# Top-k attention and a low-rank mixer on one core: the pace of the parameter conversion, two reciprocals, one step's masks and one tile's buffer

## The chip, the cores and the metric

The kernel runs on 1 core of one Trainium2 chip. The metric is the device time of one execution in microseconds (us); lower is better. Engines are named as in the profile: PE is the matrix engine, PEld its weight loads, DVE the vector engine, ACT the scalar engine, POOL the GpSimd engine, SP the queue that issues most DMAs.

## The reference

```python
# attention: batch 8, heads 8, seq 576, head_dim 64
scores = (1 / np.sqrt(64)) * np.matmul(q, k.transpose(0, 1, 3, 2))
kth = np.partition(scores, -32, axis=-1)[..., -32:-31]        # 32nd largest of a row
scores = np.where(scores >= kth, scores, -1e9)
attn = np.exp(scores - scores.max(-1, keepdims=True))
attn = attn / (attn.sum(-1, keepdims=True) + 1e-9)
out = np.matmul(attn, v)
# bridge: (B,H,S,D) -> x of (B,S,H*D) = (8, 576, 512)
# mixer: U (576,32), V (32,576), w_ch1 (512,2048), w_ch2 (2048,512)
h = x.transpose(0, 2, 1) @ U @ V
u = x + h.transpose(0, 2, 1)
result = u + np.maximum(u @ w_ch1, 0.0) @ w_ch2
```

q, k and v are float32. The four mixer parameters arrive as float64 and are handed to the kernel as pairs of 32-bit words, so that the kernel itself turns them into float32.

## The kernel before, in words

**Work units.** The heads of a batch are taken in pairs: a pair `g` is two heads of one batch, 4 pairs a batch (`NPAIR = 4`), 32 in all. The 576 query rows of a pair are cut into four tiles of 128 rows (`t` = 0 to 3) and a tail of 64 (`t = 4`). One tile has two lanes (its two heads), each of 128 rows by 576 scores; the tail of both heads together is one lane, `Stail`.

**Steps.** An outer loop over `n` runs through the list `steps`. In the first batch every tile and every tail is a step of its own, 5 a pair, so that steps 0 to 19 are the first batch (`ALONE = 20`). From step 20 on a pair has 4 steps, and the last of them holds tile 3 and the tail together, three lanes; it is called a border step here. Steps 23, 27, 31 and so on are border steps: 28 in all.

**What a step does to a tile.** PE makes the scores of the *next* step's tile (L350), ACT copies them to `Ssb` (L395, L404 to L406). DVE finds each row's 32nd largest by four rounds of an 8-fold maximum (L521, L539) with three removals between (L534); from pair 5 on it first folds the two halves of a row with POOL's help (`fold` and `split`: POOL L446 adds the halves, DVE L448 takes their maximum straight from the scores' PSUM buffers, POOL L449 subtracts), and then works on halves of 288 (L500, L502) and 304. Then come the masks: ACT scales the threshold (`least`, L565), writes a large number wherever a score is below it (L571, tile `E`), and POOL subtracts that from the scores (L572). ACT then takes the exponential and the row sum (`weigh`, L453; sums in `den`). The weights are turned, on PE (L634, L639) up to pair 5 and by DVE (L598) and a trip through DRAM after that, and PE multiplies them by V (L708, L711; copied out by ACT L720). When a pair is done, `inverse` makes the reciprocals of its sums on DVE (L651, L653) and sends them to DRAM, `scale` fetches them back spread over the partitions, POOL multiplies by them (L740, L743), and the mixer's small products follow (`mixed`).

**Order.** The instructions stand in the order in which the loop writes them, on each engine in that order; nothing moves them later. Each step's tile is followed by a generator, `front`, whose parts (`next(here)` for this step's tile, `next(last)` for the tile before) the loop calls in turn. The two-layer product of a finished batch (`mlp`, PE L845 and L862) is cut into single matmuls and dealt out between these parts by `fill`.

**Parameters.** A list `params` of 36 blocks is worked off by `next_params(1)`: each call finishes one block (DVE shift by 3 bits, L202 or L193; POOL adds L203 and L205), starts the ACT passes of the block before it (L179, L180, L183; single ones are also dealt out by `fill`) and issues the DMA of a new one (L157) into one of three `raw` buffers. With fewer than `LATE` blocks left, the shift takes the two-input form L193 instead of L202. The first batch's loop calls it twice in tiles 0 and 1, once in tiles 2 and 3; from step 20 on the calls stand behind the scores (L1312) and behind `split`.

**Buffers.** Tag `E` has two buffers. The third lane's mask goes into tag `tplace`, which has one.

Of the kernel before, what the change touches and what calls it, by code (L numbers as in the profile page):

```python
# [26 lines left out]
def kernel(  # L27
# [30 lines left out]
    P = 128  # L58
# [81 lines left out]
        return slice(h * D, (h + 1) * D)  # L140

    SLAB = 512
    LATE = 12
    spare = []


# [85 lines left out]
    def next_params(n):  # L232

        while passes:
            passes.pop(0)()
        while parts:
            f64_join(*parts.pop(0))
        while raws:
            r, outs = raws.pop(0)
            if isinstance(outs, list):  # L240
                parts.append((*f64_parts(r, None), outs))
                continue
            made = f64_parts(r, outs)
            parts.append((*made, [(made[1], same)]))
        for _ in range(min(n, len(params))):
            srcs, outs = params.pop()
            raws.append((f64_raw(srcs), outs))
# [186 lines left out]
    def split(g, t):  # L434

        if (g, t) in folds:
            pair(g, t, 1)
# [30 lines left out]
    def front(tiles):  # L468
# [92 lines left out]
        if gaps:  # L561
            slots = [lane[0] for lane in gaps]
            lo, hi = min(slots), max(slots) + 1
            least = small.tile([P, 3], F32, tag="least", name="least", bufs=3)
            nc.scalar.mul(least[:, lo:hi], m8[:, lo:hi, 7], WIDEN)  # L565
            for c, chunk, *_ in gaps:
                if c == 2:
                    gap = attn.tile([P, S], F32, tag="tplace", name="E", bufs=1)
                else:
                    gap = attn.tile([P, S], F32, tag="E", name="E")  # L570
                nc.scalar.activation(gap, chunk, AF.Relu, bias=least[:, c : c + 1], scale=-WIDEN)  # L571
                nc.gpsimd.tensor_tensor(chunk, chunk, gap, ALU.subtract)  # L572
            yield
# [615 lines left out]
    def tiles(n):  # L1189

        return steps[n] if 0 <= n < STEPS else []
# [22 lines left out]
        pass  # L1214
    scores(0, 0)
    turning = ready = iter(())
    fronts = {}
    for n in range(STEPS + 2):
        if n < STEPS:
            g, t = steps[n][0]  # L1220
            if t == 0 and g < NPAIR:
                load(g + 1)
            if t == (1 if g < NPAIR else 2) and g + 1 < NP:
                ready = prep(g + 1)
            fronts[n] = front(steps[n])
            next(fronts[n])
        else:
            t = NT
        here, last = fronts.get(n, iter(())), fronts.pop(n - 1, iter(()))
        if n >= ALONE - 1 and n <= ALONE:  # L1230

            if n < ALONE:
                next(last)
                values(*steps[n - 3][0])
                list(turning)
                next(here)
                next(last)
                scores(*steps[n + 1][0])
                fold(*steps[n + 1][0])
                values(*steps[n - 2][0])  # L1240
            list(turns(*steps[n - 1][0]))
            values(*steps[n - 1][0])
            if n < ALONE:
                split(*steps[n + 1][0])
                next(here)
                next(here)
                inverse(g, 0, 2 * NT)
                mixing.append(mixed(g, 1))
                fill()
                next(here)  # L1250
                continue
            fill()
            scores(*steps[n + 1][0])
            fold(*steps[n + 1][0])
            next(here)
            while mixing:
                fill()
            next_params(1)
            fill()
            next(last, None)  # L1260
            next(here)
            fill()
            split(*steps[n + 1][0])
            next(here)
            coming = loading(g + 1)
            next(coming)
            next(coming)
            next(here)
            fill()
            continue  # L1270
        if n < ALONE:
            ease = n > 0 and eased(*steps[n - 1][0])
            if ease:
                next(last, None)
            scores(*steps[n + 1][0])
            fold(*steps[n + 1][0])
            if n >= 3:
                values(*steps[n - 3][0])
                if (n - 3) % CH == NT:
                    mixing.append(mixed((n - 3) // CH, 3))  # L1280
            list(turning)
            fill()
            next(here)
            if t < NT - 1:
                next_params(1)
            fill()
            next(ready, None)
            next(here)
            next(last, None)
            fill()  # L1290
            split(*steps[n + 1][0])
            next(here)
            if t in (0, 1, NT - 1):
                next_params(1)
            next(here)
            fill()
            if n >= 1:
                turning = turns(*steps[n - 1][0])
            continue
        next(last, None)  # L1300
        fill()
        if ALONE <= n - 3 <= STEPS - 3:
            weighted(n - 3)
            if waiting:
                waiting.clear()
                if next(mixing[0], True):
                    mixing.pop(0)
        for tile_ in tiles(n + 1):
            if tile_[1] < NT:
                scores(*tile_, len(tiles(n + 1)) > 1)  # L1310
            fold(*tile_)
        next_params(1)  # L1312
        turn()
        fill()
        turn()
        next(last, None)
        for tile_ in tiles(n - 2):
            back(*tile_)
        fill()
        turn()  # L1320
        fill()
        next(last, None)
        if n < STEPS and n - 2 >= ALONE and len(tiles(n - 2)) > 1:
            scale(steps[n - 2][0][0])
        next(here, None)
        fill()
        if n >= STEPS:
            if n == STEPS:
                inverse(NP - 1, 0, 2 * NT + 1)
                scale(NP - 1)  # L1330
            weighted(n - 2)
        next(here, None)
        for tile_ in tiles(n + 1):
            split(*tile_)
        if t < NT - 1:
            next_params(1)
        fill()
        next(here, None)
        for tile_ in tiles(n - 1):
            if shared(*tile_):  # L1340
                blocks(*tile_)
        turning = turned(n - 1)
        if n < STEPS and n - 1 >= ALONE and len(tiles(n - 1)) > 1:
            inverse(steps[n - 1][0][0], 0, 2 * NT + 1)
        if n < STEPS:
            if t == NT - 1:
                coming = loading(g + 2) if g + 2 < NP else iter(())
            next(coming, None)
        next(ready, None)
        next(here, None)  # L1350
        fill()
        fill()
# [35 lines left out]
```

## Time and profile before

| what | value |
|---|---|
| time, three runs | 1660.09, 1662.59, 1664.67 us; median 1662.59 |
| profiled execution: time, span | 1663.47 us, 1661.4 us |
| mean granted PE clock | 0.966 |
| PE, DVE busy | 1562.3 us (94%), 1550.0 us (93%) |
| ACT, POOL busy | 991.2 us (60%), 1012.4 us (61%) |
| DMA | 189.42 MB, mean 114 GB/s |

The page cuts the span into 40 slices of 41.5 us. In the first five (the first batch) PE shows 4 to 7 tenths and the clock 7 tenths, DVE 9 from the second on; from the twelfth to the 36th PE and DVE both show 9 tenths. Then DVE falls to between 2 and 5 tenths and PE goes on alone: the last batch's two-layer product (`closing`).

### The profile page before, as it was taken

Reading aid. Unit: us, or ns where it says so; the run is one execution under the profiler, and the core shown is the slowest. Engines: PE = TensorE matmul, PEld = TensorE weight load, DVE = VectorE, ACT = ScalarE, POOL = GpSimd, SP = SyncE. Lnnn points to the kernel's source line nnn. Section 1 sums busy time; section 2 is a strip of 40 time slices with the busy share of each in tenths; the row PEclk is TensorE's granted clock in tenths of the full one; section 3 lists DMA queues with packets and bytes.
Section 4 is the critical chain, followed back from the end, with each engine's and each line's share of the span. In section 5 each row is a group of like instructions: output and inputs, shape, how many; then the busy total and the mean of one; then the engine's idle time right before and its main releaser. Section 6 shows DMA issues by size and latency. Waiting matters only on the chain.

```text
span 1661.4 us, 30244 instructions
## 1 busy us (share of the span) xinstructions
PE 1562.3 (94%) x9638; PEld 1188.0 (72%) x9638; DVE 1550.0 (93%) x4394; ACT 991.2 (60%) x2475; POOL 1012.4 (61%) x881
## 2 busy tenths in 40 slices
PE   4676698999899999999999999999999999999999
PEld 2444466787677887778777887788777877788776
DVE  7999999999999999999999999999999999994452
ACT  4888778665555666566665656566665656564320
POOL 4787669666656565666666565656666565653620
PEclk7777798999999999999999999999999999999999
DMA  3323232244545555454445555454545455543001
GB/s 88 90 82 94 67 95 74 57 128 128 136 126 140 139 144 138 133 138 131 129 130 137 132 152 133 131 138 129 131 128 140 129 154 132 134 123 110 8 2 29
DMA packets 280399, 189.42 MB, mean 114 GB/s; under 512 B 174288, under 2 KB 261168, under 8 KB 280240
## 3 DMA queue, kind: packets, MB, share of 16 engines
q1 hardware_dynamic: 259728, 117.62, 29.3%
q10 hardware_dynamic: 20512, 69.87, 13.3%
q8 instruction: 76, 1.25, 0.3%
q14 instruction: 83, 0.68, 0.1%
HBM read 116.49 MB, written 70.91 MB: 113 GB/s over the span
## 4 chain that ended last, share of the span: by engine, by line
PE 69%; DVE 20%; DMA 3%; POOL 3%; ACT 2%; SPq 2%; issue 1%; ACTq 0%; DVEq 0%; POOLq 0%
PE mm L862 22%; PE mm L845 19%; DVE m L539 7%; PE sc L350 6%; DVE upper L534 6%; PE O L711 6%; PE mm L938 3%; DVE first L521 2%; PE tp L938 2%; PE sc L938 2%; PE sc L382 2%; PE up L785 2%; DVE y L598 1%; PE O L708 1%; DVE place L534 1%
## 5 line engine op out<-in xcount | busy, mean ns | idle before, releaser
L845 PE MATMUL mm<-uT,w 128*128 128x320 f32 (+1 forms) x1792 | 465.3, 411 | 3.0 <-POOL uT L801 2.3
L862 PE MATMUL mm<-hT,w 128*128 128x320 f32 (+1 forms) x1792 | 462.0, 409 | 0.0
L572 POOL TENSOR_TENSOR Ssb<-Ssb,E 128x576 f32<-128x576 f32 x243 | 341.3, 1424 | 195.2 <-ACT E L571 195.2
L845 PEld LDWEIGHTS mm<-uT,w 128*128 128x128 f32 x1792 | 335.7, 192 | 104.2 <-issue 12.8
L862 PEld LDWEIGHTS mm<-hT,w 128*128 128x128 f32 x1792 | 333.6, 191 | 92.6 <-issue 11.1
L539 DVE MAX8 m<-upper 128x8 f32<-128x304 f32 (+1 forms) x774 | 362.7, 509 | 0.7
L534 DVE MATCH_REPLACE8 upper<-m,upper 128x304 f32<-128x304 f32 (+1 forms) x516 | 256.8, 505 | 0.0
L446 POOL TENSOR_TENSOR lower<-Ssb 128x576 uint32<-128x576 uint32 x108 | 152.8, 1415 | 133.3 <-ACT Ssb L395 71.3
L449 POOL TENSOR_TENSOR lower<-lower,upper 128x576 uint32<-128x576 uint32 x108 | 152.3, 1410 | 130.2 <-DVE upper L448 128.0
L453 ACT ACTIVATE Ssb<-Ssb,nmax 128x576 f32<-128x576 f32 x258 | 201.7, 784 | 19.4 <-POOL Ssb L545 9.8
L350 PE MATMUL sc<-qkT 64*128 64x288 f32 (+1 forms) x1056 | 177.7, 459 | 9.8 <-ACT Ssb L404 7.9
L571 ACT ACTIVATE E<-Ssb,least 128x576 f32<-128x576 f32 x243 | 176.2, 768 | 4.3
L502 DVE MAX8 upper<-lower 128x8 f32<-128x288 f32 x432 | 172.0, 439 | 4.4 <-POOL lower L449 4.4
L395 ACT COPY Ssb<-sc 128x576 f32<-128x576 f32 x216 | 127.5, 642 | 75.7 <-PE sc L350 75.7
L598 DVE STREAM_TRANSPOSE y<-Ssb 128x512 f32<-128x512 f32 (+1 forms) x312 | 154.1, 545 | 0.3 <-ACT Ssb L453 0.2
L711 PE MATMUL O<-PT,va 128*64 128x128 f32 x2048 | 143.8, 284 | 0.0
L857 ACT ACTIVATE hT<-mm 128x320 f32<-128x320 f32 (+1 forms) x224 | 91.1, 408 | 81.7 <-PE mm L845 77.5
L350 PEld LDWEIGHTS sc<-qkT 64*128 64x128 f32 (+1 forms) x1056 | 95.7, 197 | 50.1 <-issue 17.5
L711 PEld LDWEIGHTS O<-PT,va 128*64 128x64 f32 x2048 | 112.6, 140 | 16.1 <-issue 1.6
L720 ACT COPY XT<-O 128x128 f32<-128x128 f32 x128 | 34.0, 266 | 113.1 <-PE O L711 108.3
L534 DVE MATCH_REPLACE8 upper<-first,upper 128x304 f32<-128x304 f32 x216 | 97.5, 459 | 0.0
L500 DVE MATCH_REPLACE8 lower<-upper,lower 128x288 f32<-128x288 f32 x216 | 94.0, 443 | 0.0
(268 smaller groups left out, 2271.6 us busy)
## 6 DMA issues: line engine op xcount, KB each, us to landing
away<-y SPq DMA_DIRECT2D x416, 144.0 KB
PT<-away ACTq DMA_DIRECT2D x104, 576.0 KB
raw<-in_moe_w_ch_dram SPq DMA_DIRECT2D x32, 512.0 KB
va<-in_v_dram SPq DMA_DIRECT2D x64, 128.0 KB
scale<-rd ACTq DMA_DIRECT2D x56, 144.0 KB
out_dram<-ob SPq DMA_DIRECT2D x59, 128.0 KB
ld<-in_q_dram SPq DMA_DIRECT2D x108, 64.0 KB
ld<-in_k_dram SPq DMA_DIRECT2D x108, 64.0 KB
```

The lines of the kernel that those rows point to most:

```text
L350: nc.tensor.matmul(out, lhsT=qkT[half(h), 0, cols(t)], rhs=qkT[half(h), 1, lo:hi], start=True, stop=True,)
L446: nc.gpsimd.tensor_tensor(bottom, a.bitcast(U32), b.bitcast(U32), ALU.add)
L453: nc.scalar.activation(E, chunk, AF.Exp, bias=nmax, scale=SCALE, accum_out=total)
L502: nc.vector.max(spot, lower)
L534: nc.vector.match_replace(nxt, ms[c], curs[c], NEG)
L539: nc.vector.max(ms[c], curs[c])
L571: nc.scalar.activation(gap, chunk, AF.Relu, bias=least[:, c : c + 1], scale=-WIDEN)
L572: nc.gpsimd.tensor_tensor(chunk, chunk, gap, ALU.subtract)
L598: nc.vector.transpose(y[:, :, i * NT : i * NT + c].rearrange("p r c j -> p c r j"), E2[:, a : a + c * P].rearrange("p (c r j) -> p c r j", ...
L711: nc.tensor.matmul(O[half(h)], lhsT=va[:, h, j, :], rhs=PT[:, NT * h + j], start=False, stop=(j == NT - 1),)
L845: nc.tensor.matmul(phs[f][:, 0:w], lhsT=first_layer(cc, f), rhs=uT[:, cc, lo:hi], start=(cc == 0), stop=(cc == NC - 1),)
L862: nc.tensor.matmul(po[:, 0:w], lhsT=w2[:, f, c * P : (c + 1) * P], rhs=hTs[f][:, 0:w], start=(f == 0), stop=(f == NF - 1),)
```

## The change

It has five parts. (1) `next_params` is called twice in tile 2 of the first batch too (seven blocks a pair instead of six), three times in step 20 instead of once, and from step 21 on at other places: behind `next(here)` instead of behind the scores, and at the step's end instead of behind `split`, with step 23's first call left out. (2) `LATE` goes from 12 to 8. (3) The `inverse` of pairs 4 and 5 moves from the end of a step to behind the first part of the next step's `front`. (4) In step 24 the masks of step 23 (`next(last)`) move from the head of the step to behind the second `turn()`. (5) The third lane's mask takes a buffer of tag `E` like the others.

```diff
-    LATE = 12
+    LATE = 8
...
             for c, chunk, *_ in gaps:
-                if c == 2:
-                    gap = attn.tile([P, S], F32, tag="tplace", name="E", bufs=1)
-                else:
-                    gap = attn.tile([P, S], F32, tag="E", name="E")
+                gap = attn.tile([P, S], F32, tag="E", name="E")
                 nc.scalar.activation(gap, chunk, AF.Relu, bias=least[:, c : c + 1], scale=-WIDEN)
                 nc.gpsimd.tensor_tensor(chunk, chunk, gap, ALU.subtract)
...
-    fronts = {}
+    fronts, owed = {}, []
...
             next(fronts[n])
+            if owed:
+                inverse(owed.pop(), 0, 2 * NT + 1)
...
             split(*steps[n + 1][0])
+            next_params(1)
             next(here)
             coming = loading(g + 1)
             next(coming)
             next(coming)
+            next_params(1)
             next(here)
...
-            if t in (0, 1, NT - 1):
+            if t < NT:
                 next_params(1)
...
-        next(last, None)
+        slow = n == ALONE + NT
+        if not slow:
+            next(last, None)
         fill()
...
             fold(*tile_)
-        next_params(1)
         turn()
         fill()
         turn()
         next(last, None)
+        if slow:
+            next(last, None)
...
         next(here, None)
+        border = g == NPAIR and t == NT - 1
+        if not border:
+            next_params(1)
         fill()
...
         for tile_ in tiles(n + 1):
             split(*tile_)
-        if t < NT - 1:
-            next_params(1)
         fill()
...
         if n < STEPS and n - 1 >= ALONE and len(tiles(n - 1)) > 1:
-            inverse(steps[n - 1][0][0], 0, 2 * NT + 1)
+            owed.append(steps[n - 1][0][0])
+            if owed[0] > NPAIR + 1:
+                inverse(owed.pop(), 0, 2 * NT + 1)
...
         next(ready, None)
+        if t != 0:
+            next_params(1)
         next(here, None)
```

## The prediction

> **What bounds the kernel.** I read the stretches first, then the waits, then the timeline from 240 to 340 us. Columns of the stretches: us, then busy time of PE, PEld, DVE, ACT and POOL, granted PE clock, DMA share, GB/s.
>
> ```profile
> 206.00:236.00 30.00, 29.30 (x158) 20.14 (x159) 30.00 (x57) 28.84 (x66) 21.59 (x17) 1.00 0.36 106
> 248.80:253.00 4.20, 0.04 (x1) 0.04 (x1) 4.20 (x12) 2.88 (x7) 1.82 (x2) 0.79 0.00 0
> 253.00:258.00 5.00, 5.00 (x13) 3.44 (x14) 5.00 (x15) 5.00 (x12) 5.00 (x4) 0.50 0.00 0
> 258.00:282.00 24.00, 23.84 (x165) 17.40 (x163) 22.51 (x66) 22.44 (x53) 23.61 (x18) 1.00 0.44 127
> 282.00:289.00 7.00, 4.50 (x13) 2.78 (x13) 5.21 (x16) 5.26 (x12) 6.77 (x8) 0.76 0.00 0
> 289.00:331.00 42.00, 41.90 (x285) 30.69 (x284) 38.67 (x119) 25.68 (x65) 28.73 (x24) 1.00 0.21 49
> 400.00:440.00 40.00, 33.90 (x220) 24.50 (x219) 39.97 (x124) 22.57 (x59) 25.54 (x24) 0.96 0.58 154
> 500.00:1500.00 1000.00, 999.04 (x6400) 772.81 (x6401) 997.28 (x3032) 604.12 (x1532) 618.71 (x538) 1.00 0.51 135
> ```
>
> Up to about 250 us DVE is the bound (184.83 of 186 us from 20 to 206, 30.00 of 30 above). From 500 to 1500 PE never waits, and its long matmuls start every 269 or 216 ns almost without spread: PE is the bound, and DVE keeps up by 2.7 us in 1000. Whatever the change does early arrives at the end only as an earlier PE. PE's losses are in 248 to 289 and 400 to 440 us. This is where the change works:
>
> ```profile
> 250.09 0.21 ACT L565 ACTIVATE least<-m 128x3 f32<-128x3 f32 x1 [7.07 <-DVE m L539]
> 252.96 1.11 PE L634 MATMUL tp<-ident,Ssb 128*128 128x128 f32 x4 [4.18 <-ACT XT L720]
> ...
> 258.46 1.73 POOL L205 TENSOR_TENSOR w<-w,raw 128x512 uint32<-128x512 uint32 x1
> ...
> 261.60 0.82 DVE L502 MAX8 upper<-lower 128x8 f32<-128x288 f32 x2 [0.54 <-POOL lower L449]
> ...
> 284.18 0.44 PE L750 MATMUL tp<-ident,uT 128*128 128x128 f32 x2 [2.01 <-POOL uT L740]
> ...
> 287.00 0.82 DVE L502 MAX8 upper<-lower 128x8 f32<-128x288 f32 x2 [1.79 <-POOL lower L449]
> ...
> 331.03 0.76 DVE L448 TENSOR_TENSOR upper<-sc,Ssb 128x576 f32<-128x576 f32 x1 [2.15 <-ACT Stail L415]
> ```
>
> ACT stands 7.07 us before step 23's masks, which need DVE's last maximum; the copy that PE wants (L720) is queued behind them, so PE stands 4.18 us and then runs at half clock from 251.23 to 258.05. From 258 to 282 POOL is 98% busy (23.61 of 24): conversion adds (L203, L205) delay its folds, for which DVE waits, and L740, for which PE waits. At 331 DVE waits for PE.
>
> **Masks of step 23 behind two turns.** ACT's copies L720, L395 and L635 no longer stand behind L565; the masks still start when DVE is done, since ACT is idle until then. PE's 4.18 us go, and with them the half clock: 5.1 us of work at half speed, 2.55 us. But PE then meets the next gate: the scores at 262.77 need the PSUM buffers that DVE's L448 frees, which ended at 258.44. PE's work between is 9.81 − 2.55 = 7.26 us, so PE would be there at about 257 and wait. PE's gain at this point is therefore set by DVE, 262.77 against L448's new end.
>
> **Seven blocks a pair.** DVE does four more L202 before step 20, 4 × 0.41 = 1.64 us later (ends 0.40 and 0.85 each, the extremes in that stage), fully on the path, DVE being the bound there. Up to L448 of step 24 the order of before has six L193: 1.75 + 0.82 + 0.67 + 0.67 + 1.36 + 1.47 = 6.74 us. After, all eight that are left (LATE 8) stand ahead of it.
>
> ```profile
> L193 DVE SCALAR_TENSOR_TENSOR w<-w,nought x12: 667/1091/1751, 210.7 to 290.7; 128x512 uint32<-128x512 uint32 x12
> L202 DVE TENSOR_SCALAR w<-w x20: 399/408/852, 51.1 to 203.5; 128x512 uint32<-128x512 uint32 x20
> ```
>
> L193 costs 0.67 alone and about 1.45 where it starts beside POOL's mask subtracts, soon after a step's first maxima. The new places are behind the second maxima and at the step's end; I take 0.9, nearer to the rows in mid-step (258.37, 269.98, 281.60: 0.68). So 8 × 0.9 − 6.74 = +0.46, with 1.64 makes L448 of step 24 2.1 us later, at 260.5; PE starts the scores there, **2.2 us earlier** than before. Ends: at 0.67 4.1 us earlier, at 1.45 2.2 us later. The added ACT passes (two blocks of 0.68 + 0.77 + 0.77, 4.4 us more before 250) lie in the 7.07 us in which ACT stood; POOL's two pairs of adds (5.2 us) in the 8.4 us that it has free from 206 to 236. SP's `raw` DMAs wait for L205 and hold the loads behind them; the loads of pair 5 are needed at 232, so I take nothing.
>
> **Relief behind step 24.** Before, six more L193 (0.68 + 1.45 + 0.68 + 1.44 + 0.68 + 1.59 = 6.5 us) and seven pairs of POOL adds stood behind 257 us; after, no L193 and one pair. L740 then need not wait for 281.72's add, and PE's 2.01 + 0.26 + 0.22 us at 284 go, as does the half clock from 285.36 to 288.77 (1.7 us): **4.2 us**. If L740 stays late, this is nought. DVE gets ahead by its L193 and its waits for L449 (0.54 + 0.92 + 1.79), 9.8 us in all, but what PE has not won it gives back at 331, where it waits for PE already.
>
> **The clock.** Idle times of 4.18, 2.5 and 2.26 us were each followed by half clock (6.83, 3.41, 3.41 us), those of 1.06 and 1.27 at 405 and 417 were not. The new wait of up to 3.5 us before 260.5 can bring one, 1.7 to 2.55 us; ACT and POOL, fuller before 250, may stretch PE's work over it and prevent it. I charge half of the smaller: 0.85 us.
> The Trainium skill (TensorE: Matmul & The Clock Gate, "What's actually happening") has the clock fall after an idle window of about 3.4 us. The drops after 2.5 and 2.26 us speak against taking this as a threshold for one wait; by the rule the 1.7 us at 285 would have another cause and the estimate would be that much smaller.
>
> **Reciprocals.** One DVE wait ends (0.84 us before L651 at 311.55; there is none at 260.62), worth nothing at the end since DVE waits for PE at 331. The four DMAs to DRAM start some 4 us later (260.62 against L521's end at 264.7), on SP behind four more loads that were out by 265 before; pair 4's fetch may then hold ACT's queue by up to 2 us (issue at 268.41), with L640 and two L857 behind it, whose buffers PE needs only 8 us later (32 matmuls of 269 ns). Nothing.
>
> **The third mask in tag E.** It must wait for POOL's first subtract:
>
> ```profile
> 629.95 1.44 ACT L571 ACTIVATE E<-Ssb,least 128x576 f32<-128x576 f32 x2
> 630.80 2.79 POOL L572 TENSOR_TENSOR Ssb<-Ssb,E 128x576 f32<-128x576 f32 x2 [3.37 <-ACT E L571]
> 631.29 0.76 ACT L571 ACTIVATE E<-Stail,least 128x576 f32<-128x576 f32 x1
> ```
>
> The subtract ends at 632.22, so ACT stands 0.92 us, in all 28 border steps alike, with L857 (or L873), L720 and L395 behind it. In this step ACT idles 0.41 + 0.42 us before L720 and L395 anyway, and PE reused the buffer that L857 frees 3.73 us after its end (3.1 to 11.4 in the others, but one of 0.87 at 353.6); POOL's L446 starts at 634.91 behind the third subtract, not behind L395. I take 0; the other end is 0.92 × 28 = 26 us.
>
> **The sum.** 2.2 + 4.2 − 0.85 = 5.6 us. The profiled execution (span 1661.4 in 1663.47 us) comes to 1657.9; it lay 0.88 us above the median of before, so the median comes to **1657.0 us**.
>
> **Rivals.**
> *DVE's early load eats it.* L193 stays at 1.45 beside POOL, and the new PE wait costs the full half clock: −2.2 + 4.2 − 2.55 = −0.6, about 1663; between this and the forecast lies 1660. For it: POOL is fuller before 250 than before. Against: the new places.
> The Trainium skill (SBUF — State Buffer, "SBUF: two separate sides") says that VectorE and GpSimd lock a shared port pair for a whole instruction and that the other blocks; by that each of the eight could wait out a 1.3 us add, an estimate of up to 2 us each and a loss.
> *The E ring turns the sign.* ACT's 0.92 us less the 0.42 that it idles reach PE in each border step: 0.5 × 28 = 14 us, 14 − 5.6 = 8.4 slower, 1671. It decides from (5.6 + 5) / 28 = 0.38 us a step. For it: PE is the bound there with no slack of its own. Against: the 3 to 11 us of buffer slack.
> *More than forecast.* PE's idle from 400 to 440 (6.1 us, for DVE's and POOL's results) goes too: 1651. Against: DVE is tied to PE at 331.
> That the change does not do what it says can be excluded: the instruction orders show each move, and PE's order is the same in both.
>
> **Numbers.** Forecast 0.53, early load 0.27, E ring 0.15, more 0.05. About 0.3% (5 us) is what a measurement of this kernel can tell from no change. The forecast lies just beyond it (1657.6), as does the larger gain: faster 0.58; early load same 0.27; slower 0.15. The range runs from L193 at 0.67 with no half clock (1.9 + 0.85 more: 1654) and part of the 400 us idle, 1652.5, to the early load's end with a little from the ring, 1664.
>
> **What would show it.** Right: no PE wait above 1 us at step 24's first L634, PE idle below 0.5 us at L750 of pair 4, at most one half clock between 245 and 290 us, L193 x8 near 0.9 us, DVE's wait before 331 longer than 2.15 us, PE busy throughout from 500. Wrong: L193 above 1.3 us, PE waits for L720 or L857 in the border steps, or DVE idle before 250 us.

## The result

The changed kernel takes 1664.87 us (median of 22 runs, 1662.43 to 1668.36), the kernel before 1661.91 us in 22 runs on the same chips: ratio 1.0019, 95% interval 1.0012 to 1.0025, so 3.0 us slower. The forecast was 5.6 us faster; sign and range were missed. The profiled execution has a span of 1663.4 us against 1661.4. From L571 of the kernel before up to its loop, lines of the changed kernel are 3 lower: L571, L720 and L857 are L568, L717 and L854 there. The experiments keep the numbers of the kernel that they start from, and those with the third mask back in `tplace` have the numbers of the kernel before.

The same stretches as before, for the changed kernel (us, then busy time of PE, PEld, DVE, ACT and POOL, granted PE clock, DMA share, GB/s):

```profile
206.00:236.00 30.00, 25.08 (x123) 16.55 (x122) 26.82 (x52) 24.45 (x55) 21.49 (x17) 0.89 0.44 119
248.80:253.00 4.20, 4.20 (x29) 3.13 (x29) 4.20 (x11) 2.23 (x5) 1.39 (x1) 1.00 0.01 1
258.00:282.00 24.00, 20.18 (x126) 14.58 (x125) 21.28 (x70) 14.79 (x37) 19.12 (x14) 0.86 0.13 33
282.00:289.00 7.00, 7.00 (x45) 5.12 (x42) 6.02 (x16) 4.64 (x12) 4.15 (x6) 1.00 0.00 1
500.00:1500.00 1000.00, 998.42 (x6393) 769.96 (x6392) 998.10 (x3035) 604.66 (x1534) 619.70 (x538) 1.00 0.52 136
```

The two places that the change aimed at are clean: PE is busy throughout at 248.8 to 253 and at 282 to 289, though these are stretches of time, and the changed kernel is some 7 us later in its work there. New holes are at 206 to 236, where DVE, the bound of that stretch, fell from 30.00 busy us to 26.82, and at 258 to 282, where PE fell from 23.84 to 20.18 at a clock of 0.86. The steady state is as before.

To place the loss, I compare the start of each step between the two traces: DVE's first maximum of step n, and PE's scores issued in step n (times of before; changes in us, each against before's profiled execution).

```
                        DVE L521, step   20      21      25  |  PE scores L350, issued in step 24   25      26     60
kernel before (us)                    199.1   209.4   263.9  |                             262.8  275.5   291.8  687.8
changed kernel                        +1.2    +7.1    +7.3   |                             +7.5   +7.1    +2.4   +2.4
three calls -> one in step 20         +1.1    +1.1    +1.1   |                              0.0   -0.1    -4.6   -5.4
... and masks at head of step 24      +1.1    +1.1    +1.3   |                             +3.1   +2.7    -2.0   -2.0
... and masks behind the copies       +1.4    +1.4    +1.4   |                             -5.8   +1.6    -3.1   -3.2
... and POOL clear for the subtracts  +1.5    +1.5    +0.4   |                             -3.7   -2.1    -5.2   -4.8
before + masks behind the turns       +0.1    +0.1    +1.9   |                             +4.0   +3.6    +0.7   +0.6
before + masks behind the copies      -0.2    +0.5    +1.3   |                             -7.4   +4.0    +0.9   +0.5
before + masks, POOL clear            +0.2    +0.2    +0.1   |                             -3.8   -1.3    +0.1   +0.3
before + two calls in step 20         +0.1    +7.0    +8.9   |                             +8.2   +8.9    +6.9   +6.3
```

From the third row down the kernels are the experiments that follow ("..." adds to the third row's kernel). The changed kernel loses 5.9 us within step 20 and wins 4.7 us between 275 and 292 us; from there on its distance stays between 1.9 and 3.4 us, 2.4 in the last step. Each row is one execution. That of the kernel before took 1663.47 us, 1.6 above its median, so that the others look faster in the rows by about that much; how long a kernel takes is read from the medians.

Step 20 in the changed kernel's timeline (start, us, engine, line; in brackets the idle time before and what ended it):

```profile
204.69 1.19 DVE L202 TENSOR_SCALAR w<-w 128x512 uint32<-128x512 uint32 x1
...
209.22 0.28 ACT L406 COPY Ssb<-sc 128x128 f32<-128x128 f32 x1
...
210.83 0.69 ACT L179 ACTIVATE w<-raw 128x512 f32<-128x512 f32 x1
...
211.56 0.69 DVE L193 SCALAR_TENSOR_TENSOR w<-w,nought 128x512 uint32<-128x512 uint32 x1 [2.90 <-ACT w L179]
...
214.95 1.63 DVE L193 SCALAR_TENSOR_TENSOR w<-w,nought 128x512 uint32<-128x512 uint32 x1
...
216.50 1.41 DVE L521 MAX8 first<-Ssb 128x8 f32<-128x576 f32 x2
...
217.05 0.67 ACT L179 ACTIVATE w<-raw 128x512 f32<-128x512 f32 x1 [2.33 <-DMA raw<-in_moe_w_ch_dram]
...
219.84 0.74 ACT L854 ACTIVATE hT<-mm 128x320 f32<-128x320 f32 x2
...
220.31 1.97 PE L842 MATMUL mm<-uT,w 128*128 128x320 f32 x3 [4.31 <-ACT hT L854]
```

`next_params` is a line of three stations: a call runs the shift (L193) of the block that the call before converted, starts ACT's passes of the block that the call before fetched, and fetches the next. The middle call therefore puts an L193 into DVE's order whose input (L179) ACT makes only at 210.83, behind the score copies L404 to L406 and two copies of `uT`. DVE, in order, stands 2.90 us with all its maxima behind it. The step's growth adds up: L202 at 1.19 instead of 0.41 (0.78; it runs beside POOL's L755, and takes 0.41 again in the kernel with one call), the wait (2.90), and two L193 that the kernel before has in later steps (0.69 and 1.63) make 6.00 us; 7.1 − 1.2 = 5.9 were measured. The third call has its own wait: its data have not landed, ACT stands 2.33 us for them before 217.05, the copy L854 is queued behind, and PE stands 4.31 us before 220.31, with 6.83 us of half clock from 218.56.

Step 24 in the changed kernel's timeline:

```profile
256.30 1.29 POOL L203 TENSOR_TENSOR w<-w,raw 128x512 uint32<-128x512 uint32 x1 [3.27 <-DVE w L193]
...
257.67 1.29 POOL L205 TENSOR_TENSOR w<-w,raw 128x512 uint32<-128x512 uint32 x1
...
258.93 1.40 POOL L446 TENSOR_TENSOR lower<-Ssb 128x576 uint32<-128x576 uint32 x1
...
260.29 3.22 POOL L569 TENSOR_TENSOR Ssb<-Ssb,E 128x576 f32<-128x576 f32 x2
...
261.72 0.78 ACT L568 ACTIVATE E<-Stail,least 128x576 f32<-128x576 f32 x1 [2.88 <-POOL Ssb L569]
...
262.40 0.76 ACT L453 ACTIVATE Ssb<-Ssb,nmax 128x576 f32<-128x576 f32 x1
...
263.31 0.43 ACT L854 ACTIVATE hT<-mm 128x320 f32<-128x320 f32 x1
...
263.79 4.64 PE L842 MATMUL mm<-uT,w 128*128 128x320 f32 x8 [3.81 <-ACT hT L854]
263.81 0.73 DVE L448 TENSOR_TENSOR upper<-sc,Ssb 128x576 f32<-128x576 f32 x1
...
268.88 0.82 DVE L502 MAX8 upper<-lower 128x8 f32<-128x288 f32 x2 [2.69 <-POOL lower L449]
```

PE's 4.18 us at the transpose are gone, and 3.81 us at the next product have come: the third mask and the weighing (L453) wait on ACT for POOL's subtracts, those stand behind two conversion adds and the fold of the next step (L446), and the copy that PE needs (L854) stands behind the weighing. L448 ends only after PE has resumed; it isn't what PE waits for.

### The profile page after: what moved, and what is told of

It is laid out like the page before. It is cut to its first block, busy times and chain, and to the rows that moved or that the text cites. A ratio compares the mean times of both kernels' runs of the same rounds, so it can differ in the third digit from the quotient of the medians.

```text
span 1663.4 us, 30247 instructions
## 1 busy us (share of the span) xinstructions
PE 1561.3 (94%) x9638; PEld 1185.0 (71%) x9638; DVE 1547.4 (93%) x4394; ACT 992.9 (60%) x2475; POOL 1011.2 (61%) x881
## 4 chain that ended last, share of the span: by engine, by line
PE 70%; DVE 21%; DMA 3%; ACT 2%; POOL 2%; SPq 1%; issue 1%; DVEq 0%; ACTq 0%; POOLq 0%
PE mm L859 22%; PE mm L842 20%; DVE m L539 7%; PE sc L350 7%; DVE upper L534 6%; PE O L708 6%; PE mm L935 3%; DVE first L521 2%; PE sc L382 2%; PE tp L935 2%; PE sc L935 2%; PE up L782 2%; PE O L705 1%; PE tp L631 1%; DVE y L595 1%; DVE upper L502 1%
## 5 line engine op out<-in xcount | busy, mean ns | idle before, releaser
L446 POOL TENSOR_TENSOR lower<-Ssb 128x576 uint32<-128x576 uint32 x108 | 152.6, 1413 | 139.0 <-ACT Ssb L395 71.3
L453 ACT ACTIVATE Ssb<-Ssb,nmax 128x576 f32<-128x576 f32 x258 | 201.9, 785 | 18.0 <-POOL Ssb L545 9.3
L568 ACT ACTIVATE E<-Ssb,least 128x576 f32<-128x576 f32 x243 | 176.2, 768 | 4.2
L502 DVE MAX8 upper<-lower 128x8 f32<-128x288 f32 x432 | 172.1, 439 | 5.7 <-POOL lower L449 5.7
L854 ACT ACTIVATE hT<-mm 128x320 f32<-128x320 f32 (+1 forms) x224 | 91.3, 408 | 83.4 <-PE mm L842 81.0
L717 ACT COPY XT<-O 128x128 f32<-128x128 f32 x128 | 34.0, 266 | 105.9 <-PE O L708 101.9
```

The source lines that it names most:

```text
L453: nc.scalar.activation(E, chunk, AF.Exp, bias=nmax, scale=SCALE, accum_out=total)
L502: nc.vector.max(spot, lower)
```

## The experiments

All are compared with the kernel before, run beside them; ratios carry 95% intervals. "The kernel with one call" is the changed kernel with one call in step 20.

**One call in step 20.** Everything else of the change stays; the two left-out blocks are done by the calls of later steps.

```diff
             split(*steps[n + 1][0])
-            next_params(1)
             next(here)
...
             next(coming)
-            next_params(1)
             next(here)
```

> The changed kernel with one block of parameters in step 20 instead of three; all else as changed. Theory A (the burst in step 20): in the changed kernel's trace DVE stands 2.90 us at 211.56 for ACT's pass L179 and does 2.3 us of L193 there, and PE stands 4.31 us at 220.31 for ACT's copies and then runs at half clock for 6.83 us; the first maxima of step 21 come 7.1 us later than in the kernel before, of which the four earlier blocks explain 1.2. Without the two extra calls the 2.90 us and the 4.31 us go, step 21 starts 1 to 3 us later than before instead of 7.1, and most of that arrives at the end: 1660 us (1658.5 to 1662), 3 to 6 us below the changed kernel. The two blocks move to steps 23 to 25, where they cost POOL 2.6 us each. Theory B (step 24's move pays for everything): step 20's delay is swallowed by the waits of step 24, and the time stays within 1.5 us of the changed kernel, 1664 to 1666.

Measured: 1658.95 us, ratio 0.9982 (0.9973 to 0.9991), 3 us below before and 5.9 us below the changed kernel. DVE has no wait in step 20 (30.00 of 30 us busy from 206 to 236) and step 21 starts 1.1 us late instead of 7.1. The added calls are the main loss, and without them the change gains.

**The masks back at the head of step 24.**

```diff
-        slow = n == ALONE + NT
+        slow = False
```

> The changed kernel with the masks of step 23 back at the head of step 24; all else as changed. Theory A: the move replaced one PE stall by another (4.18 us for L720 and half clock in the kernel before; 3.81 us for ACT's copy L854 and 6.83 us of half clock at 262.93 in the changed one), so undoing it brings the old stall back and the time stays within 1.5 us of the changed kernel: 1663.5 to 1666.5. Theory B (the move is the loss): 3 us or more faster, below 1662. Theory C (the move gained what was forecast and others lost it): 5 us or more slower, above 1669.

Measured: 1666.96 us, 1.0031 (1.002 to 1.0043): 2.1 us above the changed kernel. PE waits 6.06 us for L717 instead of 3.81 for L854. The move is worth about 2 us in this company.

**The third mask back in `tplace`.**

```diff
-                gap = attn.tile([P, S], F32, tag="E", name="E")
+                if c == 2:
+                    gap = attn.tile([P, S], F32, tag="tplace", name="E", bufs=1)
+                else:
+                    gap = attn.tile([P, S], F32, tag="E", name="E")
```

> The changed kernel with the third lane's mask back in its own buffer; all else as changed. Theory A (the E ring costs only in step 24): ACT's wait of 2.88 us before the third mask at 261.72 goes, but the exponential behind it waits for the same subtract; 0 to 1 us faster, 1663.5 to 1665, and no shift between steps 30 and 130 against the changed kernel. Theory B (the ring costs PE something in each of 28 border steps): 0.1 to 0.4 us each, 3 to 11 us faster, and the shift against the kernel before falls step by step from 30 to 130.

Measured: 1664.24 us, 1.0016 (1.0007 to 1.0024), not to be told from the changed kernel. In the changed kernel ACT does wait for the first subtract in the later border steps, about 0.86 us each where the forecast had 0.92:

```profile
633.20 2.78 POOL L569 TENSOR_TENSOR Ssb<-Ssb,E 128x576 f32<-128x576 f32 x2 [3.37 <-ACT E L568]
634.64 0.78 ACT L568 ACTIVATE E<-Stail,least 128x576 f32<-128x576 f32 x1 [0.85 <-POOL Ssb L569]
```

But PE's distance to before is 2.4 us in step 26 and 2.4 in the last step, and with the buffer back it is 0.4 and 0.5, without a trend in either: there is no loss per border step, and the rival of the E ring is out. In step 24 alone the ring may count, as PE's wait there is 3.15 us with the buffer back instead of 3.81; the time doesn't show it.

**The reciprocals back at the end of the step.**

```diff
-            if owed[0] > NPAIR + 1:
+            if True:
                 inverse(owed.pop(), 0, 2 * NT + 1)
```

> The changed kernel with the reciprocals of pairs 4 and 5 back at the end of the step; all else as changed. Theory A: DVE waits some 0.5 to 1.5 us for the sums again, but DVE waits for PE at about 333 us anyway, so nothing arrives: 1664 to 1666. Theory B (the later fetch of the reciprocals holds ACT's queue in step 25 and delays PE): 1 to 3 us faster, 1661.5 to 1664. Theory C (the waits of DVE count): 1 us or more slower, above 1666.

Measured: 1663.91 us, 1.0014 (1.0005 to 1.0022); 1 us lower by medians, with overlapping intervals. Taken up again below.

**Two calls in step 20, without the third, and without the middle one.** Each drops one of the two lines of the first diff.

> The changed kernel with two calls for parameters in step 20 instead of three: the third (behind the loads) is left out. Theory middle: the price of the three is DVE's 2.90 us wait at 211.56, for passes of ACT that the middle call queued behind its copies; it stays, and the time stays within 1.5 us of the changed kernel: 1663 to 1665. Theory third: the price is ACT's 2.33 us wait for the third block's data and PE's 4.31 us behind it; both go, and the time falls to 1658.5 to 1660. Theory count: each call costs half of the 5.9 us that the two cost together: 1662.

> The changed kernel with two calls for parameters in step 20: the middle one (behind the split) is left out, the third stays. Theory middle: DVE's wait of 2.90 us goes and with it 4 us or more of the 5.9: 1659 to 1661. Theory third: the time stays near the changed kernel, 1663 to 1665, with ACT still waiting for the third block's data and PE behind it. Theory count: 1662.

Measured: without the third 1664.34 us, 1.0017 (1.0008 to 1.0026); without the middle one 1660.48 us, 0.9997 (0.9988 to 1.0005). Dropping the third alone wins nothing, dropping the middle alone wins about 4 us, dropping both 5.9; the third costs something only where the middle one is gone. The reason is a row of the timeline without the third:

```profile
214.06 0.69 DVE L193 SCALAR_TENSOR_TENSOR w<-w,nought 128x512 uint32<-128x512 uint32 x1 [5.43 <-ACT w L179]
```

PE's wait of 4.31 us shrank to 1.76, and DVE's grew from 2.90 to 5.43, for which DVE has one L193 less and shorter ones later; the first maxima of step 23 start at 240.4 us in both kernels. The stage is DVE's, and PE's 4.31 us and its half clock in step 20 cost nothing that shows. Without the middle call DVE has no wait there.

**The two added calls alone, in the kernel before.**

```diff
             split(*steps[n + 1][0])
+            next_params(1)
             next(here)
...
             next(coming)
+            next_params(1)
             next(here)
```

> The kernel of before with the two added calls for parameters in step 20 and nothing else of the change. Theory own term: DVE again waits about 2.9 us there for passes that ACT has queued behind its copies and does two L193 more, so that step 21 starts some 5 us later; two blocks fewer remain for the stage behind step 24, which gives back 1 to 2 us: 1664 to 1666 against about 1661.5. Rival: the 5.9 us come only beside the four added L202 and the later masks, and here the time stays within 1.5 us of before.

Measured: 1669.79 us, 1.0045 (1.0032 to 1.0059), 7.7 us slower, more than expected. DVE has the same wait, and one more in step 21, for a block that was fetched by step 20's third call and for whose data ACT stands 3.82 us:

```profile
211.42 0.69 DVE L193 SCALAR_TENSOR_TENSOR w<-w,nought 128x512 uint32<-128x512 uint32 x1 [4.63 <-ACT w L179]
226.72 0.69 DVE L193 SCALAR_TENSOR_TENSOR w<-w,nought 128x512 uint32<-128x512 uint32 x1 [2.75 <-ACT w L179]
```

The loss belongs to the calls themselves and needs no other part of the change.

**The masks' move alone, in the kernel before.**

```diff
-        next(last, None)
+        slow = n == ALONE + NT
+        if not slow:
+            next(last, None)
         fill()
...
         next(last, None)
+        if slow:
+            next(last, None)
         for tile_ in tiles(n - 2):
```

> The kernel of before with one part of the change alone: the masks of step 23 issued behind step 24's first two turns. Theory L448 (as in the forecast): PE's 4.18 us before the transpose and the half clock go, and the scores of step 24 start when DVE's L448 ends at 258.4 instead of at 262.8, 4.3 us earlier; of that 2 to 4 us arrive, 1658 to 1660 against 1662. Theory hT: the copy of PE's next product (L857) now stands behind the masks and the weighing, PE gets a new wait of 3 to 4 us there as in the changed kernel (3.81 us), and the scores come at most 1 us earlier: 1661 to 1662.

Measured: 1663.29 us, 1.0011 (1.0002 to 1.0019): slower, by 2 us. Neither expectation had this; the mechanism is that of theory hT, only larger. In its timeline of step 24:

```profile
254.63 1.28 POOL L203 TENSOR_TENSOR w<-w,raw 128x512 uint32<-128x512 uint32 x1 [0.63 <-DVE w L193]
...
257.23 3.22 POOL L572 TENSOR_TENSOR Ssb<-Ssb,E 128x576 f32<-128x576 f32 x2
...
258.67 0.77 ACT L453 ACTIVATE Ssb<-Ssb,nmax 128x576 f32<-128x576 f32 x1 [6.14 <-POOL Ssb L572]
...
261.37 3.04 PE L845 MATMUL mm<-uT,w 128*128 128x320 f32 x5 [8.72 <-ACT hT L857]
```

POOL's subtracts, now issued behind the fold and the adds of step 24, start at 257.23 although their masks were ready at 251.9; ACT stands 6.14 us, and PE 8.72 us, twice what the move removed.

**The masks behind the copies as well.** In step 24 the masks and the weighing go behind the third turn, so that ACT's `PT` copy and L854 (L857) come first; once in the kernel before, once in the kernel with one call. The diff is against the masks behind the turns.

```diff
-        next(last, None)
-        if slow:
+        if not slow:
             next(last, None)
...
         turn()
         fill()
+        if slow:
+            next(last, None)
+            next(last, None)
         next(last, None)
```

> The kernel of before, with step 23's masks issued behind ACT's copies L640 and L857 of step 24 as well, and no other part of the change. Theory copy: the 8.72 us for which PE stood for L857 when the masks went behind the turns alone come from the weighing queued ahead of it; they go, PE meets L448 (258.4) as the forecast had it, 4 us earlier than before, and the time is 1658 to 1660. Rival: the masks, 1 to 2 us later, push POOL's adds and folds and DVE's L193 behind them, and the time stays at 1660.5 to 1663.

> The changed kernel with one call for parameters in step 20, and step 23's masks issued behind ACT's copies L637 and L854 of step 24 as well. Theory copy: with one call in step 20 PE stands 4.22 us at 257.54 only because L854 is queued on ACT behind the third mask and the weighing, which wait for POOL's subtracts; in front of them it is done at about 252, the 4.22 us and the half clock (1.7 us) go, and PE meets L448's end at 258.3 instead of 262.8, 4.5 us earlier. Of that 2 to 4 us arrive: 1655 to 1657, against 1659 to 1660 for the kernel with one call. Rival: DVE and POOL hold the scores a step later and give all of it back: 1658 to 1660.

Measured: 1663.84 us, 1.0015 (1.0006 to 1.0023), and 1661.44 us, 1.0000 (0.9992 to 1.0009). Theory copy holds for one step and fails at the end. With one call in step 20, PE now does meet L448, and does start the scores of step 24 5.8 us earlier than before, as the forecast's mechanism wanted; then it stands in step 25:

```profile
258.73 0.76 PE L350 MATMUL sc<-qkT 64*128 64x288 f32 x4 [0.98 <-DVE upper L448]
259.04 0.78 ACT L453 ACTIVATE Stail<-Stail,nmax 128x576 f32<-128x576 f32 x1 [0.49 <-POOL Stail L569]
259.49 0.84 DVE L539 MAX8 m<-upper 128x8 f32<-128x304 f32 x2
...
261.75 0.75 ACT L183 ACTIVATE raw<-raw,nudge 128x512 f32<-128x512 f32 x1
262.39 0.20 ACT L565 ACTIVATE least<-m 128x2 f32<-128x2 f32 x1
...
264.29 0.25 ACT L717 COPY XT<-O 128x128 f32<-128x128 f32 x1
...
264.59 1.12 PE L631 MATMUL tp<-ident,Ssb 128*128 128x128 f32 x4 [4.52 <-ACT XT L717]
```

L717 is queued behind step 24's own masks, and ACT comes to these (L565) only at 262.39, although DVE's maxima for them ended at 260.33: the weighing of step 23, which the move put off, and a block's three conversion passes keep ACT busy without a break from 259.04 on. What PE wins in step 24 it returns a step later to ACT's order, with 6.83 us of half clock (10.24 in the other kernel, with 2.10 and 4.89 us of waits).

**The masks at the head, with one call in step 20** (the first and second diff together).

> The changed kernel with one call for parameters in step 20 and step 23's masks back at the head of step 24: what is left is seven parameters a pair without the calls close together. Theory relief: nearly all of the gain of the kernel with one call is the relief behind step 24, and the masks' place is worth at most 1 us either way: 1658 to 1660. Rival: the masks' place is worth the 2 us that it was in the changed kernel: 1661 to 1662.

Measured: 1661.41 us, 1.0003 (0.9994 to 1.0011). Against 0.9982 with the masks behind the turns: the move is worth 2 to 4 us beside the new places of the calls. Its PE wait at the transpose is 6.52 us, more than before's 4.18: ACT stands 2.99 us before the third mask, which needs a buffer of tag `E` that POOL's first subtract frees, and that subtract stands behind conversion adds. The old place became worse by the new places of the calls, by the third mask's new buffer, or by both together; no run separates the two here.

**What holds POOL's subtracts: the adds?** The kernel with one call, without the call at the end of step 23, so that no conversion adds stand ahead of the subtracts.

```diff
-        if t != 0:
+        if t != 0 and n != ALONE + NT - 1:
             next_params(1)
```

> The changed kernel with one call for parameters in step 20 and none at the end of step 23, so that POOL has no conversion adds (2.6 us) and DVE no L193 ahead of the masks' subtracts. Theory queue: in the kernel with one call in step 20 PE's 4.22 us at 257.54 come from the subtracts that stand behind those adds, through ACT's third mask and the weighing to the copy L854; the subtracts now start 2 to 2.6 us earlier, PE's wait falls below 2 us, the scores of step 24 come 3 to 4 us earlier and 2 to 4 us arrive at the end: 1655 to 1657. Rival: DVE holds PE's scores again a step later (L448, or L449 on POOL with the adds that were put off) and gives it back: 1658 to 1660.

Measured: 1659.70 us, 0.9990 (0.9981 to 0.9999), not faster than with that call. Theory queue fell in this form: PE still waits 4.14 us for L854. Its timeline of step 24 shows what was ahead of the subtracts instead:

```profile
253.22 1.41 POOL L446 TENSOR_TENSOR lower<-Ssb 128x576 uint32<-128x576 uint32 x1 [5.07 <-DVE upper L502]
...
254.57 3.23 POOL L569 TENSOR_TENSOR Ssb<-Ssb,E 128x576 f32<-128x576 f32 x2
```

POOL stands 5.07 us before the fold of step 25, which writes the single buffer `lower` that DVE's L502 of step 24 is still reading; the subtracts, whose first mask is ready at about 252, are queued behind it. At the head of the step the masks were issued before `fold`; behind the turns they are issued after it.

**Or the fold?** In step 24 the fold is issued behind the masks: with the adds kept, with the adds away as well, and, with the call for parameters behind the masks too, in the kernel before with the masks' move alone.

```diff
-            fold(*tile_)
+            if not slow:
+                fold(*tile_)
...
         next(last, None)
         if slow:
+            for tile_ in tiles(n + 1):
+                fold(*tile_)
             next(last, None)
```

> The kernel with one call in step 20, with the fold of step 25 (POOL's L446) issued behind the subtracts of step 23's masks. Theory fold: the subtracts start when the adds end (252.7) instead of at 254.0, and PE's wait for L854 falls from 4.22 to about 2.9 us. Rival (the adds alone, or DVE's maxima, set it): the wait stays at 4 us or more. At the end at most 1 to 2 us: 1657.5 to 1659.5, since a gain in step 24 was returned in step 25 before.

> The same, without the call for parameters at the end of step 23, so that POOL has neither adds nor fold ahead of the subtracts. Theory fold: they start with the masks, some 0.8 us after the first mask's start at 251.4, instead of at 254.6, and PE's wait falls from 4.14 to 1 to 2.5 us. Rival: it stays at 4 us. Time 1657 to 1660.

> The kernel before with the masks' move alone, and the fold and the call for parameters of step 24 issued behind the masks. Theory fold: POOL's subtracts start at about 251.3 instead of 257.2, ACT's 6.14 us before L453 fall below 2, PE's 8.72 us to 2 to 4, and the 2 us that the move lost are won back: 1659.5 to 1661.5 where before has 1661 to 1662. Rival: the loss came from the weighing ahead of the copy, whatever POOL does: 1663 and a PE wait above 6 us.

Measured: 1658.47 us, 0.9979 (0.9969 to 0.9988), PE's wait 3.61 us; 1658.72 us, 0.9979 (0.9969 to 0.9988), wait 1.79 us and no half clock there; 1662.91 us, 1.0004 (0.9995 to 1.0013). Adds and fold each block by themselves, so only taking both away shortens the wait by much. The times of the first two aren't told from the 0.9982 of the kernel with one call. The last kernel's timeline beside that of the move alone:

```profile
251.28 2.79 POOL L572 TENSOR_TENSOR Ssb<-Ssb,E 128x576 f32<-128x576 f32 x2 [3.80 <-ACT E L571]
...
252.73 0.78 ACT L453 ACTIVATE Ssb<-Ssb,nmax 128x576 f32<-128x576 f32 x1 [0.20 <-POOL Ssb L572]
...
255.34 2.42 PE L845 MATMUL mm<-uT,w 128*128 128x320 f32 x8 [2.67 <-ACT hT L857]
```

Six us earlier subtracts, 0.20 us of ACT's wait instead of 6.14, 2.67 us of PE's instead of 8.72. The cause of the new gate is POOL's order. The time moved less than the wait and missed the expected 1659.5 to 1661.5 us; by the intervals it isn't told from the move alone (1.0002 to 1.0019), so it isn't shown that the 2 us come from this wait: in the kernel before PE is 3.8 us ahead at the scores of step 24 and 0.1 us behind at 292 us, because it then stands 3.41 us for L740 at 284.29 instead of 2.01; and with one call the relief behind step 24 falls to 3.1 us, so that the kernel ends where it did with the wait.

**The reciprocals and the third mask's buffer once more.** In the kernel with one call, the reciprocals put back; the same with the buffer put back too; and the reciprocals put back in the kernel with the masks behind the copies.

> The changed kernel with one call for parameters in step 20 and the reciprocals where the kernel before has them; the third mask keeps its new buffer. Theory small losses: 1.0 us below the 1658.95 of the kernel with one call, 1657.5 to 1658.3. Rival: no difference, 1658.4 to 1660.

> The changed kernel with one call for parameters in step 20, with the reciprocals and the third mask's buffer as before the change. Theory small losses: the 1.0 us of the reciprocals and the 0.6 us of the buffer are real and add up; 1657 to 1658.2, where the kernel with one call had 1658.95. Rival: both are the scatter of medians: 1658.3 to 1660.

> As the kernel with the masks behind the copies and one call in step 20, and the reciprocals where the kernel before has them. Theory nothing: within 0.8 us of that kernel, as the forecast charged the reciprocals nothing. Rival: it is 1 us faster, as putting them back in the changed kernel was (1663.9 against 1664.9).

Measured: 1658.46 us, 0.9981 (0.9971 to 0.9990); 1658.93 us, 0.9982 (0.9973 to 0.9990); 1660.47 us, 0.9999 (0.9990 to 1.0008) against 1.0000 without. By ratios none of the three differs from its partner. Both parts are worth nothing that can be measured there, and the fastest kernels are those with one call in step 20 and the masks behind the turns, 3 to 4 us below before (0.9979 to 0.9982), with or without them and with or without the fold's move. `LATE` and the other new places of the calls weren't tried alone.

## Why the prediction was wrong

**Seven blocks: the failed step.** The sum priced the added blocks by their instructions and let the added ACT passes, 4.4 us, "lie in the 7.07 us in which ACT stood". Those 7.07 us are at 243 to 250; the passes of step 20 are due at 208 to 214, where ACT is 28.84 of 30 us busy. What counts for an operand of DVE is not ACT's sum of idle time but when, in its order, ACT comes to it. The row that speaks against it was the first of those shown. The L193s themselves were priced fairly: the eight took 7.65 us (0.96 each) against 7.2, the four L202 moved step 20 by 1.2 us against 1.64. In the forecast's own terms L448 of step 24 was to end 2.1 us later than before; it ended 6.1 later (264.54 against 258.44). The 4.0 us between are DVE's two waits for ACT's passes (2.90 and 0.28), for which the sum had no term, the 0.78 of one L202 and 0.45 of the L193, less the 0.4 by which the four L202 were cheaper. At the end the added calls cost 5.9 us by the first experiment, about 4 of them for the middle one. The warning sign written down, DVE idle before 250 us, is what showed.

**Masks behind the turns.** The forecast had PE 2.2 us earlier at the scores of step 24, with L448 as the next gate. Without the added calls it is 0.0 us earlier: the next gate is L854 on ACT, behind the weighing, behind POOL's subtracts, which the move put behind the fold L446 and its wait for `lower`. The forecast followed the masks on ACT ("the masks still start when DVE is done") and named L446 in another part, but not as something that the subtracts are moved past. With the copies put first PE does meet L448. Even then nothing is kept, so the step fails twice: PE's lead in step 24 is taken back in step 25, where the put-off weighing and the conversion passes hold ACT, or at L740. The forecast's "about 257" for PE's arrival is also 1 us late by its own terms (PE stood from 248.78; 248.78 + 7.26 = 256.0), but nothing rests on it. The 2 to 4 us that the move is worth beside the other parts are measured against an old place that these parts had made worse.

**Relief behind step 24.** Right: forecast 4.2 us, measured 4.7 (from +7.1 to +2.4 us; 4.5 to 4.7 in the kernels with one call, 3.1 and 3.5 where the fold goes behind the masks). No PE wait is left at L747 of pair 4. The mechanism shows best with one call in step 20, where PE starts the scores of step 25 when it did before (−0.1 us): POOL's first multiplication of pair 4 follows the fold at once and starts 3.0 us earlier. In the kernel before:

```profile
280.33 1.31 POOL L203 TENSOR_TENSOR w<-w,raw 128x512 uint32<-128x512 uint32 x1
281.72 1.70 POOL L205 TENSOR_TENSOR w<-w,raw 128x512 uint32<-128x512 uint32 x1
283.39 1.44 POOL L740 TENSOR_TENSOR uT<-XT,scale 128x256 f32<-128x256 f32 x2
```

and with one call:

```profile
278.98 1.41 POOL L446 TENSOR_TENSOR lower<-Ssb 128x576 uint32<-128x576 uint32 x1
280.35 1.44 POOL L737 TENSOR_TENSOR uT<-XT,scale 128x256 f32<-128x256 f32 x2
```

In the changed kernel itself part of the 4.7 us is owed to PE's being 7.1 us late: with the masks' move alone, where no block moved and PE is 3.6 us late, 2.9 us are won there too.

**The clock.** Charged 0.85 us. There is one half clock between 245 and 290 us as in the estimate, but of 6.83 us, and another of 6.83 at 218.56 that cost nothing in DVE's stage.

**Reciprocals and E ring.** Nothing, as forecast; the ring's other end of 26 us didn't occur. Of the rivals, DVE's early load had the right place but the wrong mechanism: L193 did not stay at 1.45 us (median 0.69). The Trainium skill's rule on the shared port pair (SBUF — State Buffer, "SBUF: two separate sides") agrees with the trace, but the rival's estimate from it, up to 2 us on each of the eight, was too high. Four L193 started while a POOL instruction ran and ended 0.55 us after it; they took 1.63, 1.24, 1.39 and, as POOL's was nearly done, 0.69 us. One took 0.69 us with POOL's add starting just behind it, and that add took 1.79 us instead of 1.3. The other three, 0.65 to 0.69 us, met no work of POOL. Of the changed kernel's timeline, an L193 ahead of a POOL add and one behind:

```profile
211.56 0.69 DVE L193 SCALAR_TENSOR_TENSOR w<-w,nought 128x512 uint32<-128x512 uint32 x1 [2.90 <-ACT w L179]
211.62 1.79 POOL L205 TENSOR_TENSOR w<-w,raw 128x512 uint32<-128x512 uint32 x1
...
214.75 1.28 POOL L205 TENSOR_TENSOR w<-w,raw 128x512 uint32<-128x512 uint32 x1
214.95 1.63 DVE L193 SCALAR_TENSOR_TENSOR w<-w,nought 128x512 uint32<-128x512 uint32 x1
```

**The sum again.** Forecast −2.2 − 4.2 + 0.85 = −5.6. With the step 24 gate (0 for 2.2) and the added calls (5.9): −4.2 + 0.85 + 5.9 = +2.6; measured +3.0. As the 5.9 was measured afterwards, this says only that no other large term is needed; that the remaining terms fit so well, with relief and half clock both larger than forecast, is partly luck.

## What to carry to other kernels

When work is added to an engine with idle time, ask not how much idle it has but what stands ahead of the new work in its order at the moment when someone needs the result; a pipeline of three engines that is called twice in quick succession makes the second call wait for the first call's stations. When a wait is removed by reordering, list every input of the waiting engine's following instructions and follow the moved work on all engines that it touches, to what it is now queued behind; and follow it into the next step too before banking an earlier start: here the put-off work took the start back there. A change of several parts is worth splitting: here one part cost 5.9 us and hid 3 us that the others gained.

## What the runs showed of the hardware

After 190 us the half clock came in lengths of 3.41, 6.83 and 10.24 us, multiples of one window (before that up to seven of them, and the last one is cut off by the end), and whether a wait brings one isn't settled by its length: PE's wait for `uT` at about 430 us (1.98 to 2.26 us) was followed by half clock in 12 of the 20 kernels traced and not in the other 8; of the waits of 1 to 1.7 us near it one was (1.67); and the 4.22 us of the kernel with one call brought 3.41 us where 3.81 brought 6.83. The Trainium skill (TensorE: Matmul & The Clock Gate, "What's actually happening") describes a free-running window of about 3.4 us; the lengths agree with it. Drops after 2 us don't fit a full idle window as a condition, and a forecast does best to give such a wait even odds of one window.
